# Raw weights staged a block earlier, v copied out before the last transpositions, score rows sent one transfer at a time

## The chip, the cores and the metric

The kernel runs on one core of a Trainium2 chip. The metric is the device time of one execution in microseconds (us); three timed runs of the kernel before gave 2346.47, 2347.64 and 2350.71 us, median 2347.64. A difference of about 0.2% (4.7 us) is what such a measurement can tell from no change.

The engines of the core are named as the profile names them: PE (matrix products; PEld its weight loads), DVE (vector), ACT (activations and copies), POOL, and SP, which here only issues transfers. ACT can issue transfers too, and an engine works through its own instructions in order, an issue among them.

## The reference

A gated sum of an attention block and a two-layer MLP on the same 2048 tokens of width 576, all in float32:

```python
x = A_x                                              # [1, 2048, 576]
g = sigmoid((x * gate_w).sum(-1, keepdims=True))
# attention, 32 heads of 18
q, k, v = split(x @ wqkv)
a = concat_heads(softmax(q @ k.T * 18 ** -0.5) @ v) @ wo
# MLP, hidden width 4608
y = layernorm(x)
b = gelu(y @ w1 + b1) @ w2 + b2
out = g * a + (1 - g) * b
```

## The kernel before

Matrix products run on float32 numbers split into a rounded high part and a rest (hi, lo), three products for one. The program has two parts.

**Opening, about 0 to 240 us.** Four token blocks of 512 tokens (`tb` 0 to 3) pass through a list `work` of 17 groups (13 in the last block): nine groups `qk_group` make q and k rows and store them to DRAM (`qk_scr`), eight groups `v_group` make v, copy it from PSUM into one of two tiles `VT` and store it (`v_scr`). Between the groups other work of the same block is placed by its number g in the list: `norm` at g = 2 to 5 (in block 0 from 5), `x_chunk` transposes the next block of x (g = 2 to 6), `y_chunk` transposes the normalised x of this block and stores it (from g = 11 in block 0, from 8 in blocks 1 and 2), and `load_x` fetches the block after next at the end. Rounds of first scores (`next_round`, line L201 on PE, L203 on DVE) begin in block 1. In the last block the last four v groups are computed side by side as `v_chunk` stages 0 to 3: each stage has matrix products into the four PSUM tiles `quad` (L907), then transpositions of normalised x (L911) whose results ACT and DVE split (L912, L913); after stage 3, `v_out` copies the four tiles out (L888 on ACT, L890 on DVE) and ACT itself issues the two stores (L891).

PSUM is shared: `transposed`, `v_chunk` and the rounds take turns in three buffers `ps_s1`, and the four banks of `ps_a` that the groups and `quad` use become `ps_s2` and `ps_w` afterwards, so the first MLP products (L474) write where `quad` was.

The MLP is a generator, `mlp()`, that is advanced by `next(stream[0])`. Its first four advances lie in block 3, at g = 2, 6, 9 and ahead of 13. The first loads raw weights into a tile `raws` of the x pool (L343, L345, L351), the second loads two more sets into the two tiles of the pool `pp` (`STAGED`), and the third splits them (ACT rounds at L374, POOL subtracts at L158). The tiles of `pp` are also the scratch (`junk`) that `norm` writes at g = 4 and 5 (L839).

**Loop, about 270 us to the end.** 32 units (pair of heads, half of the queries) of 16 steps. In each step PE makes scores (L244) into the single PSUM tile of `ps_s2`, ACT takes the exponential (L246), PE multiplies with v (L261); beside that run the rounds of the next unit, and MLP products (L474, L597) fill PE. The scheduler counts slots: `run_due` is called about four to five times a step, and `defer(n, fn)` runs fn n slots later. When the rounds of a unit are done, `s1_finish` makes four short rows of the maxima; `rows` turns them on PE (L218), ACT copies them (L220), and four transfers write them into `qa` (L113). They are issued by SP, except while SP is busy with the loads of the next block's y (`slot[0] < ybusy[0]`): then ACT issues all four, one behind the other.

Transfers take turns in eight completion counters, whichever engine issues them; an issue waits until the transfer that used its counter before has landed.

Of the kernel before, what the change touches and what calls it, by code (L numbers as in the profile page):

```python
# [16 lines left out]
P = 128  # L17
# [41 lines left out]
def gated_mix_kernel(ctx: ExitStack, tc: tile.TileContext, x, wqkv, wo, w1, b1, w2, b2, gate_w, out):  # L59
# [42 lines left out]
    def big_tile():  # L102
        return yp.tile([P, 9, TB], F32R, name="big")

    def x_tile():
        return xp.tile([P, 4 * 640], F32, name="x")
# [4 lines left out]
    def dma_r(queue, dst, src):  # L111

        queue.dma_start(dst.bitcast(F32), src)  # L113
# [91 lines left out]
    def s1_finish(u):  # L205

        m4 = M4.pop(u)
        nm = asm.tile([P, 2, 8], F32, name="nm")
        nm2 = asm.tile([P, 2, 2, 8], F32, name="nm2")
        nmh = asm.tile([P, 2, 8], F32R, name="nmh")  # L210
        nc.vector.tensor_reduce(nm, m4, axis=AX.X, op=ALU.max, negate=True)
        nc.vector.tensor_copy(nmh, nm)
        nc.vector.tensor_copy(nm2[:, :, 0, :], nmh.bitcast(F32))
        nc.vector.tensor_tensor(nm2[:, :, 1, :], nm, nmh.bitcast(F32), op=ALU.subtract)

        def rows():
            ps = psum(ps_s1)
            nc.tensor.transpose(ps[:32, :P], nm2.rearrange("p a b c -> p (a b c)"), ident)  # L218
            mr = asm.tile([32, P], F32R, name="mr", bufs=1)
            nc.scalar.activation(mr, ps[:32, :P], AF.Copy)  # L220
            qa = QA[u % 3]
            for h in range(2):
                for b in range(2):
                    r = 64 * h + 54 + b
                    k = (h * 2 + b) * 8
                    dma_r(nc.scalar if slot[0] < ybusy[0] else nc.sync,
                          qa[r:r + 1, :].rearrange("o (t n) -> o t n", n=P), mr[k:k + 8, :].bitcast(F32))
        if looped[0]:
            ROWS.append(rows)
        else:  # L230
            defer(9, rows)
# [76 lines left out]
    def mlp():  # L308
# [10 lines left out]
            return i, m, seq[i][1] * G + 2 * m  # L319


        raws = x_tile()
        R1 = raws[:, :9 * P].rearrange("p (c n) -> p c n", c=9)
        R2 = [raws[:, 9 * P + k * D:9 * P + (k + 1) * D] for k in range(2)]
        LOADED = {}
        STAGED = {}
        NQ0 = npair // NB

        def raw1(q):
            return STAGED.get((1, q), R1)  # L330

        def raw2(c):
            return STAGED[2, c] if (2, c) in STAGED else R2[c % 4]
# [13 lines left out]
        def load_w2(c):  # L347
            if (2, c) in LOADED or c >= NFC or c % 4 >= len(R2) and (2, c) not in STAGED:
                return
            LOADED[2, c] = slot[0] + (LAND - 4 if looped[0] else 4)  # L350
            nc.sync.dma_start(raw2(c), w2[c * P:(c + 1) * P, :])  # L351
# [277 lines left out]
                HT.pop((i, j))  # L629
                W2.pop((i * (G // 2) + j // 2, j % 2))  # L630

        load_w1(0)
        for c in range(2):
            load_w2(c)
        Y[0] = big_tile()
        yield 1
        for k in range(2):
            t = pp.tile([P, 2, 2, TB], F32, name="p").rearrange("p a b c -> p (a b c)")
            STAGED[1, 1 + k] = t[:, :9 * P].rearrange("p (c n) -> p c n", c=9)
            STAGED[2, 2 + k] = t[:, 9 * P:9 * P + D]  # L640
            load_w1(1 + k)
            load_w2(2 + k)
        yield 1
        prep(0)
        prep_w2(0)
# [81 lines left out]
    with ExitStack() as a:  # L727
# [85 lines left out]
        def norm(tb, stage):  # L813

            xv = x_view(tb)
            ts_ = slice(4 * tb, 4 * tb + 4)
            if stage < 2:
                for t in (2 * stage, 2 * stage + 1):
                    st6 = sm.tile([P, 2, nc.vector.BN_STATS_DIM], F32, name="st6")
                    for n in range(2):  # L820
                        nc.vector.bn_stats(st6[:, n, :], xv[:, t, n * ND:(n + 1) * ND])
                    nc.vector.bn_aggr(stats[:, tb * 4 + t, :], st6)
            if stage == 1:
                rstd = rstds[tb] = sm.tile([P, 4], F32, name="rstd")
                sd = sm.tile([P, 4], F32, name="sd")
                var = sm.tile([P, 4], F32, name="var")
                nc.vector.tensor_scalar(var, stats[:, ts_, 1], LN_EPS, None, op0=ALU.add)
                nc.scalar.activation(sd, var, AF.Sqrt)

                nc.vector.reciprocal(rstd, sd)  # L830
                nc.vector.tensor_mul(rstd, rstd, var)
                nc.vector.tensor_add(sd, sd, rstd)
                nc.vector.tensor_scalar(sd, sd, 0.5, None, op0=ALU.mult)
                nc.vector.reciprocal(rstd, sd)
            if stage >= 2:
                junk = pp.tile([P, 2, 2, TB], F32, name="p").rearrange("p a b c -> p (a b c)")
                for t in (2 * stage - 4, 2 * stage - 3):
                    tt = 4 * tb + t
                    nc.vector.scalar_tensor_tensor(junk[:, :D], xv[:, t, 0:D], 1.0, gwb, op0=ALU.mult, op1=ALU.mult,  # L839
                                                   accum_out=glog[:, tt:tt + 1])  # L840
                    if tb == NB - 1:
                        nc.vector.tensor_scalar(xv[:, t, D:], xv[:, t, 0:64], stats[:, tt, 0:1], rstds[tb][:, t:t + 1],
                                                op0=ALU.subtract, op1=ALU.mult)
                    xs = xv[:, t, 0:D]
                    nc.vector.tensor_scalar(xs, xs, stats[:, tt, 0:1], rstds[tb][:, t:t + 1],
                                            op0=ALU.subtract, op1=ALU.mult)
# [48 lines left out]
        def v_chunk(tb, stage):  # L895

            big = xT[tb]
            wh, wl = W_V
            if stage == 0:
                quad.extend(psum(ps_a) for _ in range(4))  # L900
            for c in ((0,), (1,), (2,), (3, 4))[stage]:
                for i, ps in enumerate(quad):
                    tok = slice((2 + i // 2) * P, (3 + i // 2) * P)
                    cs = slice(i % 2 * ND, (i % 2 + 1) * ND)
                    prods = ((c, wh), (c, wl), (4 + c, wh)) if c < 4 else ((8, wh), (8, wl))
                    for k, (s_, w_) in enumerate(prods):
                        nc.tensor.matmul(ps[:, :ND], big[:, s_, tok], w_[:, c, cs], start=(c == 0 and k == 0), stop=(c == 4 and k == 1))  # L907
                for cy in (c, 4 + c) if c < 4 else (8,):
                    ps = psum(ps_s1)
                    for t in range(4):  # L910
                        nc.tensor.transpose(ps[:, t * P:(t + 1) * P], x_view(tb)[:, t, 64 * cy:64 * cy + P], ident)  # L911
                    nc.scalar.activation(made[0][:, cy, :], ps, AF.Copy)  # L912
                    nc.vector.tensor_tensor(made[1][:, cy, :], ps, made[0][:, cy, :].bitcast(F32), op=ALU.subtract)  # L913
            if stage == 3:
                for i, ps in enumerate(quad):
                    v_out(tb, 2 + i // 2, i % 2, ps)

        load_w(0)
        load_x(0)
# [18 lines left out]
        for tb in range(NB):  # L938
# [3 lines left out]
            for g, (fn, args) in enumerate(work):  # L942
# [12 lines left out]
                ng = g - (N_AT if tb == 0 else 2)  # L955
                if 0 <= ng < 4:
                    norm(tb, ng)
                if tb + 1 < NB and 2 <= g < 7:
                    x_chunk(tb + 1, g - 2)
                yg = g - (11 if tb == 0 else 8)  # L960
                if 0 <= yg < 5 and tb < NB - 1:
                    y_chunk(tb, yg)
                if g == (16 if tb == 0 else 13) and tb + 2 < NB:
# [1 line left out]
                if tb == NB - 1:  # L965
                    if g == 1:
                        load_k(0, 3 * TB, S)
                    if g == 2:
                        load_q(1)
                        next(stream[0])  # L970
                    if g == 6:
                        next(stream[0])
                    if g == 9:
                        qkstack.close()
                        wp1 = mstack.enter_context(tc.tile_pool(name="m_w1", bufs=3))
                        wp2 = mstack.enter_context(tc.tile_pool(name="m_w2", bufs=4))
                        next(stream[0])

                        nc.scalar.activation(gate, glog, AF.Exp, scale=-1.0)
                    if g == 14:  # L980
                        nc.vector.tensor_scalar(gate, gate, 1.0, None, op0=ALU.add)
                        nc.vector.reciprocal(gate, gate)
                        nc.vector.tensor_scalar(gate1, gate, -1.0, 1.0, op0=ALU.mult, op1=ALU.add)
# [4 lines left out]
                    load_k(0, TB, 2 * TB)  # L988
                if tb == 2 and g == 3:
                    load_k(0, 2 * TB, 3 * TB)  # L990
                if tb == 2 and g == 13:
                    ps = psum(ps_s1)
                    nc.tensor.transpose(ps[:, :NFC], b1r, ident[:NFC, :NFC])
                    nc.vector.tensor_copy(b1t, ps[:, :NFC])
# [287 lines left out]
```

## Time and profile before

| what | value |
|---|---|
| timed runs, median (lowest to highest) | 2347.64 us (2346.47 to 2350.71) |
| the profiled execution, its own time | 2348.81 us |
| its span in the profile | 2347.0 us |
| mean granted PE clock | 0.996 |
| busy share PE / DVE / ACT / POOL | 98% / 71% / 59% / 40% |
| PE on the chain that ended last | 90% |
| DMA | 324.11 MB, mean 138 GB/s |

The span is what the profile covers; 1.8 us of the execution lie around it. PE is busy for nearly the whole span, but a busy PE may run at half clock, so the granted clock (PEclk) is read beside it. In the profile a row of the timeline gives start, duration, engine, line, operation and tiles, and in brackets the idle time ahead of it and what ended that.

### The profile page before, as it was taken

What the parts mean: (1) busy time and instruction counts of PE and PEld (TensorE: products, weight loads), DVE (VectorE), ACT (ScalarE), POOL (GpSimd) and SP (SyncE); (2) the same over time, 40 slices, a digit from 0 to 9 for tenths busy, and PEclk for the clock granted to TensorE, in tenths of its full rate; (3) what the DMA queues carried; (4) which work ended last, traced back from release to release, by engine and by line L of the source; (5) the groups of instructions that cost most, each with busy time, mean ns of one, the idle gap of its engine ahead of it and who ended that gap; (6) DMA issues with size and microseconds to landing.
All of it is one profiled execution on the core that took longest, in us unless ns stands there. A gap on an engine that the chain in (4) does not pass through costs nothing.

```text
span 2347.0 us, 50658 instructions
## 1 busy us (share of the span) xinstructions
PE 2299.5 (98%) x20601; PEld 1620.3 (69%) x20601; DVE 1661.0 (71%) x2920; ACT 1378.7 (59%) x1626; POOL 947.7 (40%) x936
## 2 busy tenths in 40 slices
PE   8999899999999999999999999999999999999999
PEld 6878666666676666666666666666666666666668
DVE  5674677777777777777767777777777777777645
ACT  4223576666665666666665666666666666666662
POOL 4002466555554433334352434443344444343320
PEclk9999999999999999999999999999999999999999
DMA  7746555545373524223364424242464333332346
GB/s 224 249 168 195 180 164 172 153 135 158 125 207 103 157 88 144 95 76 129 102 147 142 135 92 136 95 120 92 120 158 149 116 96 118 106 99 105 112 136 222
DMA packets 162078, 324.11 MB, mean 138 GB/s; under 512 B 58126, under 2 KB 85042, under 8 KB 151010
## 3 DMA queue, kind: packets, MB, share of 16 engines
q1 hardware_dynamic: 158006, 313.68, 42.6%
q10 hardware_dynamic: 3840, 7.19, 0.8%
q8 instruction: 162, 2.65, 0.5%
q14 instruction: 70, 0.57, 0.1%
HBM read 229.59 MB, written 95.16 MB: 138 GB/s over the span
## 4 chain that ended last, share of the span: by engine, by line
PE 90%; DVE 3%; DMA 2%; ACT 2%; issue 2%; POOL 1%; SPq 0%; ACTq 0%; DVEq 0%; POOLq 0%
PE ps L597 20%; PE ps L261 19%; PE ps L474 18%; PE pss L244 13%; PE ps L201 11%; PE ps L859 3%; PE ps L1160 3%; PE ps L877 1%; DVE m L203 1%; DMA x<-in_A_x_dram 1%; PE ps L777 1%; ACT p L246 0%; ACT w L374 0%; DVE p L839 0%; POOL w L158 0%
## 5 line engine op out<-in xcount | busy, mean ns | idle before, releaser
L203 DVE TENSOR_REDUCE m<-ps 128x1 f32<-128x512 f32 x2048 | 1296.6, 683 | 441.3 <-PE ps L201 440.7
L246 ACT ACTIVATE p<-pss 128x1024 f32<-128x1024 f32 x684 | 701.7, 1026 | 462.5 <-PE pss L244 448.6
L474 PE MATMUL ps<-big,w 64*128 64x512 f32 x3834 | 515.6, 393 | 2.6 <-ACT vt L888 2.6
L597 PE MATMUL ps<-w,hh 64*128 64x288 f32 x4352 | 499.4, 300 | 12.7 <-ACT z L497 0.8
L158 POOL TENSOR_SCALAR zz<-zz 128x512 f32<-128x512 f32 x272 | 169.2, 622 | 845.3 <-ACT zz L558 776.0
L244 PE MATMUL pss<-qa,ka 56*128 56x512 f32 x2048 | 482.6, 437 | 10.4 <-ACT p L246 6.3
L246 ACT ACTIVATE ring<-pss 128x1024 f32<-128x1024 f32 x340 | 348.9, 1026 | 232.7 <-PE pss L244 223.3
L201 PE MATMUL ps<-ka,qa 54*128 54x512 f32 x2048 | 456.1, 409 | 2.7 <-DVE m L203 1.6
L597 PEld LDWEIGHTS ps<-w,hh 64*128 64x128 f32 x4352 | 400.8, 186 | 68.5 <-issue 42.5
L474 PEld LDWEIGHTS ps<-big,w 64*128 64x128 f32 x3834 | 391.7, 185 | 60.8 <-ACT vt L888 2.9
L244 PEld LDWEIGHTS pss<-qa,ka 56*128 56x128 f32 x2048 | 196.8, 184 | 265.6 <-ACT p L246 132.1
L158 POOL TENSOR_TENSOR zz<-zz,z 128x512 f32<-128x512 f32 x280 | 361.3, 1291 | 38.9 <-ACT zz L560 13.9
L597 PE MATMUL ps<-w,hl 64*128 64x288 f32 x2176 | 350.3, 293 | 0.0
L261 PE MATMUL ps<-p,vt 128*32 128x512 f32 x2736 | 344.5, 598 | 0.0
L201 PEld LDWEIGHTS ps<-ka,qa 54*128 54x128 f32 x2048 | 242.3, 185 | 28.6 <-DVE m L203 9.1
L597 PEld LDWEIGHTS ps<-w,hl 64*128 64x128 f32 x2176 | 235.1, 186 | 0.4
L158 POOL TENSOR_TENSOR w<-x,w 128x576 fp32r<-128x576 f32 (+1 forms) x34 | 67.9, 2010 | 302.5 <-DMA p<-in_B_w_dram 168.7
L158 POOL TENSOR_TENSOR hl<-zz,hh 128x512 fp32r<-128x512 f32 x134 | 174.2, 1300 | 16.7 <-ACT hh L523 5.8
L261 PE MATMUL ps<-ring,vt 128*32 128x512 f32 x1360 | 179.1, 598 | 0.0
L261 PEld LDWEIGHTS ps<-p,vt 128*32 128x32 f32 x2736 | 71.4, 109 | 147.5 <-issue 147.5
L576 DVE SCALAR_TENSOR_TENSOR x<-ps,x 128x288 f32<-128x288 f32 x270 | 110.7, 452 | 30.9 <-PE ps L597 17.7
L859 PE MATMUL ps<-big,wqk 128*128 128x512 f32 x504 | 123.8, 400 | 1.5 <-DVE wqk L771 1.2
(121 smaller groups left out, 1402.4 us busy)
## 6 DMA issues: line engine op xcount, KB each, us to landing
w<-w_scr SPq DMA_DIRECT2D x54, 1152.0 KB
w<-w_scr SPq DMA_DIRECT2D x108, 576.0 KB
w_scr<-w SPq DMA_DIRECT2D x18, 1152.0 KB
w_scr<-w SPq DMA_DIRECT2D x36, 576.0 KB
qa<-qk_scr SPq DMA_DIRECT2D x192, 72.0 KB
ka<-qk_scr SPq DMA_DIRECT2D x90, 144.0 KB
x<-in_B_w_dram SPq DMA_DIRECT2D x34, 288.0 KB
qk_scr<-hh SPq DMA_DIRECT2D x36, 256.0 KB
```

Source lines behind the costliest of these rows:

```text
L158: fn(*args, **kw)
L201: nc.tensor.matmul(ps, qa[r0:r0 + 54, t * P:(t + 1) * P], ka[r0:r0 + 54, kb * TB:(kb + 1) * TB], start=True, stop=True)
L203: nc.vector.tensor_reduce(M4[u][:, h, t, kb:kb + 1], ps, axis=AX.X, op=ALU.max)
L244: nc.tensor.matmul(ps[:, h, :], ka[r0:r0 + 56, kc * P:(kc + 1) * P], qa[r0:r0 + 56, qb * TB:(qb + 1) * TB], start=True, stop=True)
L246: nc.scalar.activation(RING[n % 3][:, qb], ps, AF.Exp, scale=SCALE)
L261: nc.tensor.matmul(OB[u][r:r + 32, :], v[:, k, 19 * h:19 * h + 32], RING[c % 3][:, qb, h, :], start=(k == 0), stop=(k == NT - 1))
L474: nc.tensor.matmul(ps[h], wt[w_][r, c, :], Y[s_][r, c, :], start=(k == 0), stop=(k == 26))
L576: nc.vector.scalar_tensor_tensor(dst, ps[nn][:, :ND], 0.5, b2b[:, cs[nn]] if base else dst, op0=ALU.mult, op1=ALU.add)
L597: nc.tensor.matmul(ps[nn][:, :ND], h_[r, tok], w_[p_][r, cs[nn]], start=(k == 0 or bare and k == 3 * G), stop=(k == 6 * G - 1 or bare and ...
L777: nc.tensor.transpose(ps[:, t * P:(t + 1) * P], x_view(tb)[:, t, c * P:(c + 1) * P], ident)
L859: nc.tensor.matmul(ps, w_[:, c, ms], big[:, s_, :], start=(k == 0), stop=(k == len(prods) - 1))
L1160: nc.tensor.matmul(ps[t, n][:, :ND], OT[b][3][:, s_, tok], w_part(w_, c)[:, cs], start=(c == 0 and k == 0), stop=(c == 4 and k == 1))
```

## The change

Six edits go together.

1. The two sets of raw weights for `pp` are loaded by the first advance of `mlp()`, which moves to block 2, g = 6; the loads into `raws` come with the second advance, at block 3, g = 2, where they were. The advance at block 3, g = 6 is gone.
2. `norm` gets a scratch tile of its own (`junk`, in the pool `sm`), since the tiles of `pp` are now held from block 2 on.
3. In `v_chunk` stage 3, all products come first, then the four copies of `v_out`, then the last three transpositions.
4. The four row transfers that ACT issues are deferred to 1, 3, 5 and 7 slots later, one each. Those that SP issues stay together.
5. In block 1, `x_chunk` runs at g = 4 to 8 instead of 2 to 6.
6. In block 0, `y_chunk` runs from g = 12 instead of 11, so its last piece falls to the last group.

```diff
@@ s1_finish / rows
-            for h in range(2):
-                for b in range(2):
-                    r = 64 * h + 54 + b
-                    k = (h * 2 + b) * 8
-                    dma_r(nc.scalar if slot[0] < ybusy[0] else nc.sync,
-                          qa[r:r + 1, :].rearrange("o (t n) -> o t n", n=P), mr[k:k + 8, :].bitcast(F32))
+            aside = slot[0] < ybusy[0]
+
+            def store(h, b):
+                r = 64 * h + 54 + b
+                k = (h * 2 + b) * 8
+                dma_r(nc.scalar if aside else nc.sync,
+                      qa[r:r + 1, :].rearrange("o (t n) -> o t n", n=P), mr[k:k + 8, :].bitcast(F32))
+            for k in range(4):
+                if aside:
+                    defer(1 + 2 * k, lambda k=k: store(*divmod(k, 2)))
+                else:
+                    store(*divmod(k, 2))
@@ mlp
-        raws = x_tile()
-        R1 = raws[:, :9 * P].rearrange("p (c n) -> p c n", c=9)
-        R2 = [raws[:, 9 * P + k * D:9 * P + (k + 1) * D] for k in range(2)]
+        R1, R2 = {}, []
+
+        def open_raws():
+            raws = x_tile()
+            R1[0] = raws[:, :9 * P].rearrange("p (c n) -> p c n", c=9)
+            R2.extend(raws[:, 9 * P + k * D:9 * P + (k + 1) * D] for k in range(2))
...
-        load_w1(0)
-        for c in range(2):
-            load_w2(c)
-        Y[0] = big_tile()
-        yield 1
         for k in range(2):
             t = pp.tile([P, 2, 2, TB], F32, name="p").rearrange("p a b c -> p (a b c)")
             STAGED[1, 1 + k] = t[:, :9 * P].rearrange("p (c n) -> p c n", c=9)
             STAGED[2, 2 + k] = t[:, 9 * P:9 * P + D]
             load_w1(1 + k)
             load_w2(2 + k)
+        yield 1
+        open_raws()
+        load_w1(0)
+        for c in range(2):
+            load_w2(c)
+        Y[0] = big_tile()
         yield 1
@@ norm
-                junk = pp.tile([P, 2, 2, TB], F32, name="p").rearrange("p a b c -> p (a b c)")
+                junk = sm.tile([P, D], F32, name="junk", bufs=1)
@@ v_chunk
-            for c in ((0,), (1,), (2,), (3, 4))[stage]:
+            cs_ = ((0,), (1,), (2,), (3, 4))[stage]
+            for c in cs_:
                 for i, ps in enumerate(quad):
...
+            if stage == 3:
+                for i, ps in enumerate(quad):
+                    v_out(tb, 2 + i // 2, i % 2, ps)
+            for c in cs_:
                 for cy in (c, 4 + c) if c < 4 else (8,):
...
-            if stage == 3:
-                for i, ps in enumerate(quad):
-                    v_out(tb, 2 + i // 2, i % 2, ps)
@@ the loop over token blocks
-                if tb + 1 < NB and 2 <= g < 7:
-                    x_chunk(tb + 1, g - 2)
-                yg = g - (11 if tb == 0 else 8)
+                xg = g - (4 if tb == 1 else 2)
+                if tb + 1 < NB and 0 <= xg < 5:
+                    x_chunk(tb + 1, xg)
+                yg = g - (12 if tb == 0 else 8)
...
-                        next(stream[0])
-                    if g == 6:
                         next(stream[0])
...
+                if tb == 2 and g == 6:
+                    next(stream[0])
```

**ACT at the end of block 3.** These are the rows of ACT before, from the last rounding of a staged weight (`w<-p`) to the first MLP row (`z<-ps,b1t`):

```order
94 L374 ACTIVATE w_2201<-p 128x1152
95 L912 ACTIVATE big<-ps 128x512 x3
96 L888 ACTIVATE vt_109<-ps 128x8x2x18
97 L891 DMA v_scr<-vt_109 128x832
98 L888 ACTIVATE vt_110<-ps 128x8x2x18
99 L891 DMA v_scr<-vt_110 128x832
100 L497 ACTIVATE z<-ps,b1t 128x512
```

And the same place in the changed program, whose line numbers are some ten higher:

```order
94 L383 ACTIVATE w_2201<-p 128x1152
95 L898 ACTIVATE vt_109<-ps 128x8x2x18
96 L901 DMA v_scr<-vt_109 128x832
97 L898 ACTIVATE vt_110<-ps 128x8x2x18
98 L901 DMA v_scr<-vt_110 128x832
99 L927 ACTIVATE big<-ps 128x512 x3
100 L506 ACTIVATE z<-ps,b1t 128x512
```

The two copies of v and their stores stand ahead of the three copies of transposed x instead of behind them; the rounding of the staged weights has not moved.

**ACT in the loop, where it issues the rows.** Before, at the first of the two places where this happens (`mr` holds the rows, `pss` the scores):

```order
382 L220 ACTIVATE mr<-ps 32x128
383 L113 DMA qa_104<-mr 1x8x128 x4
384 L246 ACTIVATE p<-pss 128x1024 x3
385 L246 ACTIVATE ring_2263<-pss 128x1024 x2
386 L374 ACTIVATE w_8752<-x 128x576
```

And after the change:

```order
382 L220 ACTIVATE mr<-ps 32x128
383 L113 DMA qa_104<-mr 1x8x128
384 L252 ACTIVATE p<-pss 128x1024
385 L113 DMA qa_104<-mr 1x8x128
386 L252 ACTIVATE p<-pss 128x1024
387 L113 DMA qa_104<-mr 1x8x128
388 L252 ACTIVATE p<-pss 128x1024
389 L113 DMA qa_104<-mr 1x8x128
390 L252 ACTIVATE ring_2263<-pss 128x1024 x2
```

One transfer now stands ahead of each of four exponentials. Of the eight exponentials of these four steps seven follow `mr` before the unit that needs the rows begins, so the last transfer is issued four exponentials, two steps, ahead of that.

More of the change, by code (lines that the diff above doesn't have):

```diff
@@ L329, in raw1 @@
         def raw1(q):
-            return STAGED.get((1, q), R1)
+            return STAGED[1, q] if (1, q) in STAGED else R1[0]
         def raw2(c):
@@ L835, in norm @@
             if stage >= 2:
-                junk = pp.tile([P, 2, 2, TB], F32, name="p").rearrange("p a b c -> p (a b c)")
+                junk = sm.tile([P, D], F32, name="junk", bufs=1)
                 for t in (2 * stage - 4, 2 * stage - 3):
                     tt = 4 * tb + t
-                    nc.vector.scalar_tensor_tensor(junk[:, :D], xv[:, t, 0:D], 1.0, gwb, op0=ALU.mult, op1=ALU.mult,
+                    nc.vector.scalar_tensor_tensor(junk, xv[:, t, 0:D], 1.0, gwb, op0=ALU.mult, op1=ALU.mult,
                                                    accum_out=glog[:, tt:tt + 1])
```

## The prediction

> **What bounds the kernel now.** I read the page's totals first, then who PE waited for, then the timeline around each long wait, then the granted clock in short windows behind them.
>
> ```profile
> span 2347.0 us, 50658 instructions
> PE 2299.5 (98%) x20601; PEld 1620.3 (69%) x20601; DVE 1661.0 (71%) x2920; ACT 1378.7 (59%) x1626; POOL 947.7 (40%) x936
> ...
> PE ps L777 <- DMA x<-in_A_x_dram: 8.7, 3, 6.0
> PE pss L244 <- ACT p L246: 6.3, 7, 2.2
> PE ps L911 <- DVE big L913: 3.2, 1, 3.2
> PE ps L474 <- ACT vt L888: 2.6, 1, 2.6
> ```
>
> PE is busy for 2299.5 of 2347.0 us, and the work on it does not change: the same products and transpositions in a slightly different order. So the change can win only from PE's 47.5 idle us and from time in which PE runs slowly. The waits (us in total, times, longest) name only a handful of stalls over 2 us; apart from the first 6.0 us, ahead of all work, the diff bears on each of the long ones. The sum is therefore one over stalls, each with the slow clock behind it. The columns of these windows are the window, its length, busy us of PE, PEld, DVE, ACT and POOL, then the granted PE clock, the DMA share and GB/s:
>
> ```profile
> 227.00:232.00 5.00, 4.93 (x27) 4.92 (x28) 3.49 (x8) 2.60 (x5) 2.94 (x2) 0.66 1.03 287
> 238.00:242.00 4.00, 3.62 (x18) 2.92 (x20) 0.23 (x1) 0.33 (x1) 0.00 (x0) 0.57 0.54 213
> 272.00:280.00 8.00, 7.82 (x55) 6.21 (x57) 4.38 (x8) 5.58 (x9) 3.81 (x3) 0.57 0.55 80
> 712.00:717.00 5.00, 4.91 (x41) 3.91 (x42) 2.07 (x5) 1.98 (x3) 0.00 (x0) 0.66 0.00 0
> 1219.00:1224.00 5.00, 4.91 (x56) 3.37 (x58) 2.96 (x6) 4.11 (x5) 2.85 (x4) 1.00 0.62 152
> ```
>
> Length times (1 - clock) is the time lost: 5 x 0.34 = 1.70, 4 x 0.43 = 1.72, 8 x 0.43 = 3.44, 1.70 and 0 us. The first two windows follow the stalls at 224 and 236 us, the fourth the one at 709; behind that at 1217 nothing was lost.
>
> **Part 1: raw weights loaded in block 2 (with the scratch tile).** The stall at 224 us:
>
> ```profile
> SPq L343 <- DMA v_scr<-vt: 7.3, 1, 7.3
> ...
> 211.35 8.54 SPq L343 DMA_DIRECT2D p<-in_B_w_dram  x2
> 220.81 1.03 PE L911 MATMUL ps<-ident,x 128*128 128x128 f32 x8
> ...
> 225.12 0.68 ACT L374 ACTIVATE w<-p 128x576 fp32r<-128x576 f32 x1 [6.25 <-DMA p<-in_B_w_dram]
> 225.71 1.07 ACT L912 ACTIVATE big<-ps 128x512 fp32r<-128x512 f32 x2
> 226.32 1.29 DVE L913 TENSOR_TENSOR big<-ps,big 128x512 fp32r<-128x512 f32 x2 [6.47 <-ACT big L912]
> 227.07 0.66 PE L911 MATMUL ps<-ident,x 128*128 128x128 f32 x4 [3.19 <-DVE big L913]
> ```
>
> SP hung 8.54 us in the second staged set behind a v store; the set came late; ACT stood 6.25 us in the rounding L374, with the copies L912 queued behind; DVE and, for a free `ps_s1` buffer, PE waited for those. With the loads some 60 us earlier ACT waits for nothing here. What is late next: the buffer PE wants needs L912 and L913 of the first transpositions, 1.07 + 1.29 us behind the transpositions that start at 220.81, so about 223.5, and PE comes at 223.88 (227.07 - 3.19). So the whole 3.19 us go, and the 1.70 us of clock behind: **4.9 us** (from 0 if another wait takes the place, to 4.9).
>
> In their new place the eight loads stand on SP between the q and k stores of block 2:
>
> ```profile
> 136.00:160.00 24.00, 23.03 (x96) 15.89 (x95) 21.20 (x47) 5.72 (x11) 0.00 (x0) 1.00 0.30 109
> ...
> 210.00 0.62 SPq L345 DMA_DIRECT2D p<-in_B_w_dram  x1
> ...
> p<-in_B_w_dram SPq DMA_DIRECT2D x4, 288.0 KB
> p<-in_B_w_dram SPq DMA_DIRECT2D x2, 256.0 KB
> ...
> 121.66 3.46 PE ps L859 x14
> 182.54 9.80 PE ps L859 x42
> ```
>
> DMA is busy for 0.30 there. Both sets are about 1.7 MB (4 x 288 + 2 x 256 KB and two small ones); at the 287 GB/s of the window 227 to 232 that is 6 us of transfers. Eight issues at about 0.6 us are 5 us on SP. Behind them wait the stores of the next groups, whose source tiles rotate in six. Block 2 lasts from 121.66 to 182.54 (first products of blocks 2 and 3 on the chain) and takes 14 such tiles, one in 4.3 us, so a store may be some 26 us late before ACT, then PE, feels it. Cost 0, up to 5 if SP's issues were exposed. The scratch tile is written by the same DVE rows: 0.
>
> **Part 2: v copied out before the last transpositions.**
>
> ```profile
> 233.21 1.03 PE L911 MATMUL ps<-ident,x 128*128 128x128 f32 x8
> ...
> 235.14 0.60 PE L911 MATMUL ps<-ident,x 128*128 128x128 f32 x4
> ...
> 236.27 0.41 ACT L888 ACTIVATE vt<-ps 128x288 f32<-128x288 f32 x1
> ...
> 237.91 0.42 ACT L888 ACTIVATE vt<-ps 128x288 f32<-128x288 f32 x1 [1.23 <-issue]
> 238.38 2.93 PE L474 MATMUL ps<-big,w 64*128 64x512 f32 x12 [2.64 <-ACT vt L888]
> ```
>
> PE is done at 235.74 and waits until ACT's second copy ends at 238.33, because L474 writes the bank that this copy reads. ACT had to do the last three L912 first, then a copy, an issue that waits for DVE's copy, and the second copy: 2.06 us from 236.27. After the change that same 2.06 us chain starts when the first `quad` tile is complete, six products before PE ends them, and PE still has twelve transpositions to make, 1.03 + 0.60 = 1.6 us. Six products at the transpositions' pace (1.03 / 8 = 0.13 us) are 0.8 us, so the second copy lands some 1.3 us after PE's last product, inside the 1.6. L912 now comes behind, but L474 takes the transposed pieces in order and needs the late ones only after twelve of its products (2.93 x 0.57 = 1.7 us at full clock). So 2.64 + 1.72 = **4.4 us** (0 to 4.4).
>
> **Part 3: rows one at a time.**
>
> ```profile
> L113 ACTq DMA_DIRECT2D qa<-mr x8: 627/630/1225, 706.7 to 1217.0; - x8
> ...
> 706.72 3.27 ACTq L113 DMA_DIRECT2D qa<-mr  x4
> 710.03 1.02 ACT L246 ACTIVATE p<-pss 128x1024 f32<-128x1024 f32 x1 [3.34 <-DMA qa<-mr]
> 711.11 0.50 PE L244 MATMUL pss<-qa,ka 56*128 56x512 f32 x2 [2.23 <-ACT p L246]
> ...
> 1217.64 1.02 ACT L246 ACTIVATE ring<-pss 128x1024 f32<-128x1024 f32 x1 [2.74 <-DMA qa<-mr]
> 1218.72 0.51 PE L244 MATMUL pss<-qa,ka 56*128 56x512 f32 x2 [2.20 <-ACT ring L246]
> ```
>
> ACT issues rows at only these two places, eight transfers in all, at 0.63 us each but for the first. Four in a row hold an exponential 3.34 and 2.74 us, and PE, with one score tile, 2.23 and 2.20 us. One issue ahead of each exponential holds it 0.63 us at most. PE's slack there is 3.34 - 2.23 = 1.1 us at the first place, so nothing is left; at the second it is 2.74 - 2.20 = 0.54, so 0.1 remains for the first issue, and 0.2 or so for each of the other three, which also share ACT with the tanh rows: 0.6. Gain 2.23 + 1.70 and 2.20 - 0.6: **5.5 us** (bounds 0 and 6.1). The 512 steps fill the span from about 270 us on, 4.0 us each, with two exponentials: the last row leaves three exponentials or 6 us later than now, and the unit that reads it begins four exponentials or 8 us after that, which a transfer of a few KB should not need. A transfer that ACT issues must also find its completion counter free; for seven of the eight the one before is long landed, and the last follows a y load issued some 10 us before.
>
> **Part 4: the two shifts in blocks 0 and 1.**
>
> ```profile
> 52.70 0.33 PE L777 MATMUL ps<-ident,x 128*128 128x128 f32 x1 [0.35 <-DVE x L845]
> 53.99 0.33 PE L777 MATMUL ps<-ident,x 128*128 128x128 f32 x1 [0.96 <-DVE x L845]
> ...
> 76.57 0.66 PE L777 MATMUL ps<-ident,x 128*128 128x128 f32 x4 [1.44 <-DMA x<-in_A_x_dram]
> ...
> 91.45 0.60 PE L777 MATMUL ps<-ident,x 128*128 128x128 f32 x4
> ...
> 93.99 0.69 DVE L795 TENSOR_TENSOR big<-ps,hh 64x512 fp32r<-64x512 f32 x1
> ```
>
> One v group more ahead of the transpositions (fourteen products at 0.13 us, 1.8 us) covers the 0.35 + 0.96 us but for 0.1: gain 1.2. Two groups later (2 x 3.46 us by the row of block 2 above) x has landed: gain 1.44. The load of x for block 2 now waits for one more transposition, and goes out about 1 us later; 7 us cover that. But the last `x_chunk` of block 1 now shares g = 8 with the first `y_chunk` and a round: four tiles in three buffers. The fourth waits for L795, 93.99 + 0.69 - 91.45 = 3.2 us after its transposition in this row, where DVE was still on `norm`; I take 2.3 without that (the 1.07 + 1.29 us of two such copies and a subtraction), against 1.3 us of PE work between (two transposition rows and a product). That is 1.05 (0 to 1.9). Sum of part 4: **+1.6 us** (0.7 to 2.6).
>
> **The sum.** 4.9 + 4.4 + 5.5 + 1.6 = 16.4 us. From the profiled execution's 2348.81 us that leaves 2332.4. The median of the timed runs is 1.2 us below that execution, about what one more or less slow stretch costs, so I forecast **2332 us** for the median.
>
> [...]
>
> **The rivals.**
> - *The clock does not come back.* The slow stretches may hang on where a stall falls; the one at 272 us stands behind no wait of over 2 us, and all stages there move by some 11 us. Then the 1.70 + 1.72 + 1.70 = 5.1 us stay, here or elsewhere: 2348.8 - 11.3 = 2337.5. The three that follow stalls speak against it. The same doubt works downward: without the 272 us stretch it is 2332.4 - 3.4 = 2329.
> - *A new wait takes the place at 224 us.* ACT could stand in the rounding of the sets that still load in block 3, or POOL's subtractions be late for L474. For it: those loads stay on a busy SP. Against: ACT did not wait for them before. Loses part 1: 2337.3.
> - *The rows do nothing*, as each single issue still hits an exponential without slack: 4 x 0.63 us lost at each place again. Loses part 3: 2337.9.
> - *Slower: SP jams in block 2.* If the eight loads held SP so long that the six rotating tiles run out, ACT, then PE, would stall there. It decides from 26 us of hold on, and to end above 2352.3 it must add some 20 us beyond: 46 us. SP's longest hold of this kind was 8.54 us with DMA at 1.0; here DMA is at 0.30.
>
> **How the numbers follow.** The forecast, all parts within their bounds (2328.5 to 2335.5): 0.50. Clock stays: 0.20. New wait: 0.12. Rows: 0.06. Several of these together, leaving less than 4.7 us (0.2%, about what a measurement can tell from no change): 0.07. Slower: 0.05. Faster is 0.50 + 0.20 + 0.12 + 0.06 = 0.88. The range 2328 to 2340 takes in the first four cases, with a little lost at each edge.
>
> **What would show it.** Right: no PE wait of L911 on L913, none of L474 on L888, none over 0.5 us of L244 near 707 and 1215 less the shift; no L374 behind a transfer; x landed ahead of L777; clock 1.0 around the v chunks. Wrong: an L374 row that still names a transfer, an L201 in block 1 waiting far over 1 us, SP rows of many us at 150, or new stretches of clock 0.5.

## The result, and the profile after

Six timed runs of the changed kernel gave a median of 2333.31 us (2332.89 to 2333.87), six of the kernel before beside them 2347.65 us (2346.47 to 2350.71): ratio 0.9934, 95% interval 0.9924 to 0.9943, so 14.3 us or 0.6% faster. The profiled execution took 2333.75 us (span 2332.0), 15.06 us less than that of before. The runs also scatter less: 1.0 us from lowest to highest instead of 4.2.

The page's totals of the changed kernel, then who PE waited for (us in total, times, longest):

```profile
span 2332.0 us, 50662 instructions
...
PE 2295.1 (98%) x20601; PEld 1613.1 (69%) x20601; DVE 1661.4 (71%) x2920; ACT 1378.4 (59%) x1626; POOL 947.8 (41%) x936
```

```profile
PE ps L787 <- DMA x<-in_A_x_dram: 7.3, 2, 6.2
PE pss L250 <- ACT p L252: 4.3, 7, 1.1
PE ps L201 <- DVE m L203: 1.6, 1, 1.6
...
PE ps L201 <- DVE big L805: 1.1, 1, 1.1
...
PE ps L1173 <- DVE big L1113: 0.6, 1, 0.6
```

No wait of over 2 us is left but the first load, and the transpositions' wait for DVE and that of the MLP's first product for `vt` are gone. One wait of 1.1 us is new (L201 on L805, block 1). Where the time came from, by the starts of the same instructions in the two profiled executions:

| place | before | after | gained so far |
|---|---|---|---|
| first product of block 1 | 65.18 | 63.44 | 1.74 |
| first product of block 2 | 121.59 | 119.90 | 1.69 |
| first MLP product (L474, now L483) | 238.38 | 229.14 | 9.24 |
| maxima turned (L218), first place of the rows | 706.10 | 695.96 | 10.14 |
| the same, second place | 1214.28 | 1200.53 | 13.75 |
| end of the span | 2347.0 | 2332.0 | 15.0 |

The end of the attention opening, in the timeline of the changed kernel:

```profile
217.08 0.67 ACT L383 ACTIVATE w<-p 128x576 fp32r<-128x576 f32 x1
...
224.86 2.90 PE L918 MATMUL ps<-wv,big 128*128 128x288 f32 x20
...
227.00 0.42 ACT L898 ACTIVATE vt<-ps 128x288 f32<-128x288 f32 x1 [0.15 <-PE ps L918]
227.60 1.47 PE L926 MATMUL ps<-ident,x 128*128 128x128 f32 x12
228.67 0.42 ACT L898 ACTIVATE vt<-ps 128x288 f32<-128x288 f32 x1 [1.25 <-PE ps L926]
229.14 1.66 PE L483 MATMUL ps<-big,w 64*128 64x512 f32 x12
...
230.87 1.09 PE L201 MATMUL ps<-ka,qa 54*128 54x512 f32 x2
```

The rounding of the staged weights (L383) waits for nothing. The second copy of v ends at 229.09, 1.33 us behind the last product (224.86 + 2.90 = 227.76), and PE transposes until 229.07: L483 starts at 229.14, with no margin to spare. One pair of score products at 230.87 then takes 1.09 us, where such a pair takes 0.40 elsewhere.

The staged loads in their new place, on SP in block 2:

```profile
153.01 2.57 SPq L352 DMA_DIRECT2D p<-in_B_w_dram  x2
...
156.98 1.29 SPq L352 DMA_DIRECT2D p<-in_B_w_dram  x2
...
158.99 0.58 SPq L360 DMA_DIRECT2D p<-in_B_w_dram  x1
```

They hold SP from 153.01 to 159.57, 6.6 us in all and 2.57 at most, far from the 26 us of cover; PE waits for nothing new there. The rows in the loop, ACT first, then PE at the two places:

```profile
696.58 1.23 ACTq L113 DMA_DIRECT2D qa<-mr  x1
697.86 1.03 ACT L252 ACTIVATE p<-pss 128x1024 f32<-128x1024 f32 x1 [1.31 <-PE ps L201]
697.89 0.67 ACTq L113 DMA_DIRECT2D qa<-mr  x1
699.48 1.02 ACT L252 ACTIVATE p<-pss 128x1024 f32<-128x1024 f32 x1 [0.59 <-PE pss L250]
699.49 0.63 ACTq L113 DMA_DIRECT2D qa<-mr  x1
...
698.94 0.50 PE L250 MATMUL pss<-qa,ka 56*128 56x512 f32 x2 [0.19 <-ACT p L252]
...
1202.97 0.50 PE L250 MATMUL pss<-qa,ka 56*128 56x512 f32 x2 [0.20 <-ACT ring L252]
```

PE's 2.23 and 2.20 us have become 0.19 and 0.20. Behind the second place 15.8 us were gained (a score row at 1204.94 for 1220.71); the end gives 0.8 back, and the new wait of L1173 is 0.6 us.

The granted clock (last columns: clock, DMA share, GB/s) behind the old stalls, and where it is still low:

```profile
227.00:232.00 5.00, 4.77 (x35) 3.54 (x35) 3.41 (x8) 2.42 (x5) 2.57 (x1) 1.00 0.43 170
...
261.00:269.00 8.00, 7.03 (x43) 5.56 (x43) 4.21 (x9) 5.88 (x9) 3.81 (x3) 0.57 0.70 106
701.00:706.00 5.00, 5.00 (x52) 3.04 (x50) 3.77 (x7) 2.74 (x3) 0.00 (x0) 1.00 0.00 1
```

Three of the four slow stretches are gone; the fourth (8 x 0.43 = 3.4 us) only moved, from 272 to 261 us. It stands in every profile of this study.

### The profile page after: what moved, and what is told of

Its sections match the earlier page's. It is cut to its first block, busy times and chain, and to the rows that moved or that the text cites. A ratio compares the mean times of both kernels' runs of the same rounds, so it can differ in the third digit from the quotient of the medians.

```text
span 2332.0 us, 50662 instructions
## 1 busy us (share of the span) xinstructions
PE 2295.1 (98%) x20601; PEld 1613.1 (69%) x20601; DVE 1661.4 (71%) x2920; ACT 1378.4 (59%) x1626; POOL 947.8 (41%) x936
## 4 chain that ended last, share of the span: by engine, by line
PE 92%; DVE 2%; issue 2%; ACT 2%; DMA 1%; POOL 1%; ACTq 0%; SPq 0%; DVEq 0%; POOLq 0%
PE ps L606 20%; PE ps L267 20%; PE ps L483 18%; PE pss L250 13%; PE ps L201 11%; PE ps L869 4%; PE ps L1173 2%; PE ps L887 2%; DVE m L203 1%; PE ps L787 0%; ACT p L252 0%; ACT w L383 0%; DMA x<-in_A_x_dram 0%; PE ps L918 0%; POOL w L158 0%
## 5 line engine op out<-in xcount | busy, mean ns | idle before, releaser
L483 PE MATMUL ps<-big,w 64*128 64x512 f32 x3834 | 514.5, 392 | 0.1
L201 PE MATMUL ps<-ka,qa 54*128 54x512 f32 x2048 | 457.8, 409 | 4.0 <-DVE m L203 1.6
L483 PEld LDWEIGHTS ps<-big,w 64*128 64x128 f32 x3834 | 388.7, 185 | 59.9 <-ACT vt L898 0.3
L201 PEld LDWEIGHTS ps<-ka,qa 54*128 54x128 f32 x2048 | 243.2, 185 | 31.3 <-DVE m L203 8.9
L585 DVE SCALAR_TENSOR_TENSOR x<-ps,x 128x288 f32<-128x288 f32 x270 | 110.7, 451 | 29.6 <-PE ps L606 16.4
```

The costliest lines, as they stand in the source:

```text
L201: nc.tensor.matmul(ps, qa[r0:r0 + 54, t * P:(t + 1) * P], ka[r0:r0 + 54, kb * TB:(kb + 1) * TB], start=True, stop=True)
L483: nc.tensor.matmul(ps[h], wt[w_][r, c, :], Y[s_][r, c, :], start=(k == 0), stop=(k == 26))
L585: nc.vector.scalar_tensor_tensor(dst, ps[nn][:, :ND], 0.5, b2b[:, cs[nn]] if base else dst, op0=ALU.mult, op1=ALU.add)
```

## The experiments

Medians in us, the number of runs, and the kernel before on the same chip beside them. That figure names three groups of measurements (2346.77, 2347.37 and 2348.77 us); it differs by 2 us between them, so across groups the ratios are compared:

| run | kernel | median (runs) | before (runs) | ratio, 95% |
|---|---|---|---|---|
| e1_rows | before + rows one at a time | 2341.66 (11) | 2346.77 (33) | 0.9975 [0.9966, 0.9984] |
| e2_stage | before + staging in block 2 | 2344.17 (11) | 2346.77 (33) | 0.9990 [0.9981, 0.9999] |
| e3_vout | before + v copied out earlier | 2345.52 (11) | 2346.77 (33) | 0.9993 [0.9985, 1.0002] |
| e4_shift | before + the two shifts | 2347.33 (11) | 2346.77 (33) | 1.0000 [0.9991, 1.0008] |
| e8_both | before + staging + v | 2341.31 (10) | 2347.37 (15) | 0.9972 [0.9963, 0.9982] |
| e5_rows_back | changed - rows | 2340.02 (6) | 2347.37 (15) | 0.9969 [0.9957, 0.9980] |
| e10_v_back | changed - v | 2335.88 (5) | 2347.37 (15) | 0.9953 [0.9941, 0.9966] |
| e11_stage_back | changed - staging | 2337.00 (5) | 2347.37 (15) | 0.9957 [0.9943, 0.9970] |
| e12_shift_back | changed - shifts | 2334.82 (5) | 2348.77 (9) | 0.9939 [0.9926, 0.9953] |
| e6_x3 | changed, x one group earlier | 2331.46 (5) | 2348.77 (9) | 0.9927 [0.9915, 0.9939] |
| e9_stalls | changed + 28 stalls | 2474.41 (1) | | |

### One part alone, on the kernel before

Each takes one part of the diff shown above as it stands. e1_rows, the rows:

```diff
...
+            for k in range(4):
+                if aside:
+                    defer(1 + 2 * k, lambda k=k: store(*divmod(k, 2)))
...
```

> The kernel before with only the rows aside going one transfer at a time. My theory (a stall of 2.2 us of PE at each of two places, one of them with 1.7 us of slow clock behind it): 5.5 us faster, about 2342 us, no score product waiting over 0.5 us near 707 and 1215 us. Rival (each single issue holds its exponential as the four did): 0 us, about 2347.6. Middle (the waits go but the slow clock turns up elsewhere): 3.8 us faster.

5.1 us faster; no score product waits over 0.5 us at either place, and no slow clock stands there. As expected.

e2_stage, the staging and the scratch tile:

```diff
...
+                if tb == 2 and g == 6:
+                    next(stream[0])
...
+                junk = sm.tile([P, D], F32, name="junk", bufs=1)
```

> The kernel before with only the raw weights staged in block 2 and the scratch tile of its own. My theory: the 3.19 us stall at 224 us and the 1.70 us of clock behind it go, 4.9 us faster, about 2342.7 us; the stall at the v copies (2.6 us) stays. Rival 1 (another wait takes the place): 0. Rival 2 (the slow clock stays, since the stall at the v copies follows 12 us later and may catch it): 3.2 us faster.

2.6 us faster by the medians (interval 0.2 to 4.5), about half of what was expected. In its profile the stall at 224 us is gone and the one for `vt` stays (2.64 us) with a slow stretch behind it; the first MLP product comes at 232.88, 5.5 us earlier than before, of which 0.9 were already gained at the start of block 3, where x landed earlier in that execution.

e3_vout, v's copies:

```diff
...
+            if stage == 3:
+                for i, ps in enumerate(quad):
+                    v_out(tb, 2 + i // 2, i % 2, ps)
             for c in cs_:
...
```

> The kernel before with only v's last copies ahead of the last transpositions. My theory: 2.64 us of stall and 1.72 us of clock go, 4.4 us faster, about 2343.3 us; the stall of the transpositions at 224 us (3.2 us) stays. Rival (ACT, late from the late weights, is still behind, so the first product of attention waits for its copies or the transposed pieces all the same): 0 to 2 us.

1.25 us faster, which can't be told from none. The wait for `vt` is gone, that of the transpositions stays (2.5 us) with its slow stretch, and this profile has another stall near the end (1.85 us, L1162 on DVE) with 1.7 us of clock behind it. That wait has 0.6 us in the changed kernel's profile and 1.0 in e6_x3; no edit bears on it.

e4_shift, the shifts:

```diff
+                xg = g - (4 if tb == 1 else 2)
+                if tb + 1 < NB and 0 <= xg < 5:
+                    x_chunk(tb + 1, xg)
+                yg = g - (12 if tb == 0 else 8)
```

> The kernel before with only the two shifts in blocks 0 and 1. My theory: 1.2 us in block 0 and 1.44 in block 1, less a new wait of about 1.1 us for a fourth score tile: 1.6 to 1.9 us faster, about 2346 us. Rival (everything behind moves against the clock's window, and slow stretches come or go): anything from 2 us slower to 5 us faster, with the waits after 200 us as before.

0.6 us slower, with an interval of 2 us to either side: inconclusive. Its block 1 starts at 63.41 as in the changed kernel, and it has the new wait of 1.1 us.

The four add up to 5.1 + 2.6 + 1.25 - 0.6 = 8.4 us, not 14.3. Each bears an error of about 2 us, since the kernel before scatters by 6.6 us over its 33 runs. Whether the rest is error or the parts help each other was the next question.

### Two parts together, and the changed kernel without one part

e8_both joins the edits of e2_stage and e3_vout; the others take one part out of the changed kernel, where the base is steady.

```diff
...
+                if tb == 2 and g == 6:
+                    next(stream[0])
...
+            if stage == 3:
+                for i, ps in enumerate(quad):
+                    v_out(tb, 2 + i // 2, i % 2, ps)
```

> The kernel before with two parts together: the raw weights staged in block 2 (with the scratch tile), and v's last copies ahead of the last transpositions. Alone they gave 2.6 and 1.25 us by the medians. If the parts simply add up as measured alone: 3.9 us faster, about 2343. My theory (each alone leaves the other's stall, with 1.7 us of slow clock behind it for certain, and together there is no stall left between 200 and 240 us): 9.3 us by the prediction's terms, 8.2 by the places of the changed kernel's rows, about 2338.5.

6.1 us faster (interval 4.2 to 8.7). That lies between the 3.9 of the two alone and my 8.2; the interval takes in 8.2, and the 3.9 have an error of some 3 us, so the run does not decide between them. Its profile has no stall and no slow clock between 200 and 240 us.

e10_v_back undoes the edit of e3_vout:

```diff
...
-            if stage == 3:
-                for i, ps in enumerate(quad):
-                    v_out(tb, 2 + i // 2, i % 2, ps)
...
```

> The changed kernel with v's last copies behind the last transpositions again. Theory: 2.64 us of stall and 1.7 us of clock come back: 4.4 us slower than the changed kernel, about 2337.7. Rival (the parts only add what they add alone): 1.3 us slower, 2334.6.

2.6 us slower than the changed kernel by the medians, between the two expectations. The stall is back to the digit (its row of the timeline), but no slow clock follows it (windows of 3.41 us: length, busy PE, PEld, DVE, ACT and POOL, clock, DMA share, GB/s):

```profile
231.80 1.67 PE L483 MATMUL ps<-big,w 64*128 64x512 f32 x12 [2.64 <-ACT vt L898]
```

```profile
227.32:230.73 3.41, 1.83 (x16) 1.59 (x13) 2.51 (x5) 1.69 (x4) 1.99 (x1) 1.00 0.00 0
230.73:234.15 3.42, 2.35 (x20) 1.95 (x22) 0.93 (x3) 0.42 (x1) 0.00 (x0) 1.00 0.63 249
```

e11_stage_back undoes the edits of e2_stage:

```diff
...
-                if tb == 2 and g == 6:
-                    next(stream[0])
```

> The changed kernel with all raw weights loaded in block 3 again, and the scratch in the shared buffer. Theory: the stall of the transpositions on DVE's subtractions comes back with 2.5 to 4.1 us, as in the profiles of the kernel before and of three experiments, and 1.7 us of clock: 4.2 to 5.8 us slower than the changed kernel, about 2338.3. Rival (the parts only add what they add alone): 2.6 us slower, 2336.

3.7 us slower by the medians. Its profile, 2.3 us above its median, has a stall of 3.65 us (timeline) and half clock in two windows behind it:

```profile
225.63 1.11 PE L922 MATMUL ps<-ident,x 128*128 128x128 f32 x4 [3.65 <-DVE big L924]
```

```profile
221.19:224.60 3.41, 0.79 (x7) 0.55 (x5) 0.00 (x0) 0.92 (x2) 0.80 (x2) 1.00 0.86 300
224.60:228.01 3.41, 2.38 (x11) 2.39 (x12) 2.39 (x4) 2.77 (x5) 2.79 (x2) 0.50 0.86 233
228.01:231.43 3.42, 3.42 (x17) 3.40 (x17) 1.85 (x5) 0.66 (x2) 1.11 (x1) 0.50 0.66 246
```

SP stands 7.88 us in the second staged set there, as it stood 8.54 us before. The trace shows what held it (timeline, then SP's waits):

```profile
209.46 7.88 SPq L349 DMA_DIRECT2D p<-in_B_w_dram  x2
...
214.32 0.35 ACTq L897 DMA_DIRECT2D v_scr<-vt  x1
```

```profile
SPq L349 <- DMA v_scr<-vt: 6.7, 1, 6.7
```

The second transfer of that row waits for the completion counter that the v store of ACT uses. ACT issues this store only at 214.32; its last packet lands at 216.73, and SP goes on at 216.75. Before it is the same: issued at 216.22, landed at 219.28, SP at 219.30. So SP stood behind a counter that came free late, in a window with a DMA share of 0.74 before, not behind full queues.

e5_rows_back undoes the edit of e1_rows:

```diff
...
-                if aside:
-                    defer(1 + 2 * k, lambda k=k: store(*divmod(k, 2)))
...
```

> The changed kernel with the four rows issued in a row again. Theory (a stall of 2.2 us at each of two places, slow clock of 1.7 us behind the first only, as in all five profiles that have these stalls): 5.6 us slower than the changed kernel, about 2339, and the slow stretch stands behind the first place again, not the second. Rival (the slow clock hangs on where a stall falls against a free-running window): 4 to 7.6 us, and either place may have it.

6.7 us slower by the medians. Both stalls are back, and here the slow clock stands behind both places, which refutes my theory that it belongs to the first (timeline, then windows):

```profile
700.62 0.79 PE L244 MATMUL pss<-qa,ka 56*128 56x512 f32 x2 [2.24 <-ACT p L246]
...
1208.20 0.50 PE L244 MATMUL pss<-qa,ka 56*128 56x512 f32 x2 [2.21 <-ACT ring L246]
```

```profile
697.24:700.65 3.41, 1.17 (x17) 0.83 (x14) 1.99 (x4) 1.02 (x1) 2.66 (x3) 1.00 0.04 10
700.65:704.07 3.42, 3.33 (x22) 2.80 (x24) 0.00 (x0) 1.02 (x1) 0.00 (x0) 0.50 0.00 0
1205.82:1209.24 3.42, 1.21 (x14) 0.89 (x12) 1.41 (x3) 1.52 (x2) 1.88 (x2) 1.00 0.65 134
1209.24:1212.65 3.41, 3.33 (x26) 3.02 (x26) 1.29 (x2) 2.26 (x4) 2.11 (x3) 0.50 0.64 168
```

e12_shift_back undoes the edits of e4_shift:

```diff
-                xg = g - (4 if tb == 1 else 2)
-                if tb + 1 < NB and 0 <= xg < 5:
-                    x_chunk(tb + 1, xg)
+                if tb + 1 < NB and 2 <= g < 7:
+                    x_chunk(tb + 1, g - 2)
-                yg = g - (12 if tb == 0 else 8)
+                yg = g - (11 if tb == 0 else 8)
```

> The changed kernel without the two shifts in blocks 0 and 1. By the places of the rows: block 1 starts 1.7 us later again, the transpositions of block 1 wait 0 to 1.5 us for x (0, 0.5, 0.7, 1.4 and 1.5 us in the five profiles that have this order), and the 1.1 us wait of the score product goes: 0.6 to 2.1 us slower than the changed kernel, about 2334.6. Rival (the shifts bring nothing, as their run alone had it): 0.

1.5 us slower by the medians, as expected, though the intervals of the two ratios overlap. Taken out one at a time the parts are worth 3.7 + 2.6 + 6.7 + 1.5 = 14.5 us by the medians, against 14.3 for the whole. These medians come from different groups; by the ratios, each against the kernel before beside it, they are 5.4 + 4.5 + 8.2 + 1.2 = 19.3 us against 15.5, each with an error of some 3 us. So taken out one at a time the parts add up within their errors. Put in alone they give 9.9 us by the ratios, 5.6 less than the whole, which is about the combined error of these five figures (some 5 us). Whether the parts help each other by a few us thus stays open.

### How long a stall slows the clock

e9_stalls repeats exponentials at 28 steps; `full` and `half` come from a list of seven sizes.

```diff
         nc.scalar.activation(RING[n % 3][:, qb], ps, AF.Exp, scale=SCALE)
+        full, half = STALLS.get((n, qb), (0, 0))
+        for _ in range(full):
+            nc.scalar.activation(RING[n % 3][:, qb], ps, AF.Exp, scale=SCALE)
+        if half:
+            nc.scalar.activation(RING[n % 3][:, qb, 0], ps[:, 0], AF.Exp, scale=SCALE)
```

> The changed kernel with exponentials computed a second to sixth time at 28 places among the 512 steps, so that the score product behind them waits; nothing else changes, and the values stay the same. An extra exponential takes ACT about 1.0 us, half of one 0.6, and PE has about 1.1 us of slack, so seven sizes of stall of about 1.0, 1.5, 2.0, 2.6, 3.0, 3.6 and 4.0 us come four times each. Theory A (a stall of over about 2 us can be followed by 1.7 us of half clock, by where it falls against a free-running window; the longer, the likelier): none behind 1.0 and 1.5 us, some behind 2.0 to 3.0, all or nearly all behind 3.6 and 4.0. [...] Theory C (it hangs on the place in the program, not on length): no order by length. Time: the stalls add some 70 us and the clock 1.7 us for each slow stretch.

The stalls came out longer than planned, 0.73 to 4.99 us and 93 us in all; the time was 2474.41 us in a single execution, 141 us more than the changed kernel's profiled execution. What stood behind each:

| stall, us | number | no slow clock | one slow window | two slow windows |
|---|---|---|---|---|
| 0.73 to 1.90 | 4 | 4 | | |
| 2.21 to 2.95 | 8 | 2 | 5 | 1 |
| 3.33 to 3.42 | 4 | | 4 | |
| 3.76 to 4.00 | 4 | | 1 | 3 |
| 4.32 to 4.99 | 8 | | | 8 |

That is theory A in its order, and more exact: in this run the granted 0.50 comes in whole windows of 3.41 us. By that, as an estimate, a window that is busy throughout loses 1.71 us, and what is idle in it loses nothing. PE was busy for 97.0 of the 116.1 us of the slow windows, so the clock cost 48.5 us and not 58. With it the time closes: PE's idle time rose by 92.3 us and its busy time by 48.3, together the 141. A second slow window followed where the stall reached at least 0.60 us into the first (all 12 cases), and none where it reached at most 0.32 us into it (the other 10). All 22 slow stretches begin on one grid with a period of 3.413 us, over 1090 us of execution, within 0.05 us. Cut along that grid, three stalls of 2.51, 2.36 and 3.89 us read:

```profile
1238.94:1242.35 3.41, 1.84 (x16) 1.39 (x14) 2.73 (x5) 2.82 (x3) 0.00 (x0) 1.00 0.51 107
1242.35:1245.77 3.42, 2.48 (x20) 1.64 (x24) 0.56 (x1) 2.17 (x4) 0.00 (x0) 1.00 1.00 367
1522.25:1525.66 3.41, 1.57 (x20) 1.22 (x16) 2.82 (x5) 3.20 (x4) 3.16 (x5) 1.00 0.22 50
1525.66:1529.08 3.42, 2.82 (x18) 2.38 (x20) 0.00 (x0) 1.49 (x2) 0.62 (x1) 0.50 0.44 129
...
1689.50:1692.91 3.41, 0.00 (x0) 0.00 (x0) 0.84 (x2) 3.31 (x4) 0.00 (x0) 1.00 0.00 0
1692.91:1696.33 3.42, 3.34 (x16) 2.68 (x18) 0.00 (x0) 1.05 (x2) 0.00 (x0) 0.50 0.00 0
```

The first window is idle for 3.41 - 1.84 = 1.57 us, and the next runs at full clock; the third is idle for 1.84 us, and the next runs at half. Among all full-speed windows of this stretch none idle up to 1.57 us was followed by half clock, and all from 1.84 us on were. (In the other profiles windows with up to 1.65 were not and those with 1.74 in e2_stage and 1.75 in e8_both were; against this order one with 1.57 in e4_shift was, so the records leave the limit open by some 0.1 us. The stretch near 261 us is left aside here.) So a stall cost clock here where about 1.7 us of it, half a window, fell into one window of the grid. From that limit I estimate that a stall of d us between 1.7 and 3.4 costs clock at a share d / 3.41 of its positions on the grid, which is 0.75 at 2.55 us: six of the eight from 2.21 to 2.95 had it.

The two places of the kernel before, on that execution's own grid:

```profile
709.29:712.70 3.41, 1.50 (x16) 1.23 (x18) 0.71 (x2) 2.05 (x2) 1.26 (x1) 1.00 0.02 3
712.70:716.12 3.42, 3.42 (x30) 3.25 (x28) 1.29 (x2) 1.02 (x1) 0.00 (x0) 0.50 0.00 0
1214.46:1217.87 3.41, 2.05 (x21) 1.61 (x20) 2.48 (x4) 0.67 (x3) 3.16 (x4) 1.00 1.06 229
1217.87:1221.28 3.41, 2.48 (x28) 2.12 (x30) 0.36 (x1) 2.46 (x4) 0.89 (x2) 1.00 0.26 56
```

At the first the stall puts 1.91 idle us into one window, at the second only 1.36, as it is cut in two. e10_v_back's two windows above, with 1.58 and 1.07 idle us, are the same case.

### Block 1's transpositions of x one group earlier

The new wait of 1.1 us in block 1 comes from four score tiles in one group with three buffers. One group earlier for `x_chunk` avoids it:

```diff
-                xg = g - (4 if tb == 1 else 2)
+                xg = g - (3 if tb == 1 else 2)
```

> The changed kernel with block 1's transpositions of x one group earlier (groups 3 to 7, not 4 to 8), so that no group has four score tiles to share three buffers. Theory: the wait of 1.1 us of a score product on a subtraction goes, and x has landed in time all the same: 1.1 us faster than the changed kernel, about 2332.2. Rivals: x comes late again (up to 0.5 us lost of it), or the wait moves to another group: 0.

2331.46 us (2331.15 to 2332.42), 1.85 us below the changed kernel's median with no overlap of their runs, though these come from different groups and the intervals of their ratios overlap. Within its own group it is 3.4 us below e12_shift_back, the same kernel without the shifts, with no overlap. Its waits have no L201 on L805, x landed in time, and block 2 starts at 118.20 instead of 119.90. So the places show the 1.1 us as gained; the times alone do not prove it against the changed kernel. The place in the changed kernel, then in this one:

```profile
96.26 0.50 PE L201 MATMUL ps<-ka,qa 54*128 54x512 f32 x1
97.88 0.50 PE L201 MATMUL ps<-ka,qa 54*128 54x512 f32 x1 [1.12 <-DVE big L805]
```

```profile
95.66 0.60 PE L787 MATMUL ps<-ident,x 128*128 128x128 f32 x4
96.19 0.49 PE L201 MATMUL ps<-ka,qa 54*128 54x512 f32 x2
```

## Why the prediction held, point by point

- **The whole.** From the profiled execution 16.4 us were to go and 15.06 went; the median came out 1.3 us above the 2332 of the forecast, whose step from 2332.4 takes off only 0.4 of the 1.2 us that it names. A sum over a handful of stalls with their clock was the right account: busy PE fell by 4.4 us (2299.5 to 2295.1), idle PE by 10.6 (47.5 to 36.9). In the timed runs the mean granted clock rose from 0.9966 (33 runs) to 0.9983 (6 runs), some 4 us of 2347, against 5.1 in the sum.
- **Part 1, 4.9 us.** The stall and its slow clock went, nothing took the place, and SP had room. Taken back it costs 3.7 us. The prediction's reading of SP's hold was off: the DMA share over those 8.54 us is 0.74, not 1.0, and the hold was a wait for a completion counter. The term rested on one execution: the same stall measures 3.19 us there and 2.49, 2.51, 3.65 and 4.10 in four others.
- **Part 2, 4.4 us.** The chain ran as worked out: the second copy lands 1.33 us behind the last product (predicted 1.3), but PE's transpositions end 1.31 us behind it instead of 1.6, so the stall is gone with nothing in hand. Taken back it costs 2.6 us, about the stall alone: the 1.72 us of clock behind it were there in three of the five profiles that have this stall (2.64 us each time), not always. This is the term that was mis-sized.
- **Part 3, 5.5 us.** 3.6 and 2.0 us at the two places by the table of places, 5.1 us alone, 6.7 when taken back. The clock behind the first place was counted as certain and behind the second as nothing; it is a matter of the grid at both. With it in six of six profiles at the first and one of six at the second, the sum came out right by luck, for a reason that I did not have. The 0.6 us kept for exposed issues was too much: PE waits 0.20.
- **Part 4, 1.6 us.** 1.5 when taken back, but by other pieces: block 0 gave 1.74 instead of 1.2 us (the 1.8 us of products there were enough for the whole 1.31, with no 0.1 to take off); the 1.44 us wait for x in block 1 was one of six outcomes from 0 to 1.53 (mean 0.8); the new wait cost 1.12 (1.05 predicted). The shift in block 1 as written thus gains nothing; one group earlier it does.
- **The rivals.** The clock came back to full at each of the three places, so the first falls, in its form that slow stretches move elsewhere; its doubt, that they hang on where a stall falls, was right. No new wait came at 224 us, the rows did bring their gain, and SP did not jam. The shortcoming is the clock's price: 1.7 us or nothing by chance, not 1.7 for sure.

## What to carry to other kernels

Where one engine is busy for 98% of the span, list its few stalls of over 2 us and find for each what stands ahead of the awaited operation on its engine; that is what to move. Price a stall in full, and the slow clock behind it by the chance that enough of it falls into one window of the clock's grid (here, by e9_stalls, an estimated d / 3.41 for a stall of d us between 1.7 and 3.4; the stretch near 261 us aside, no full-speed window of any profile with under 1.57 idle us had half clock behind it). Where runs scatter, judge small parts by taking them out of the steadier kernel, and measure what is compared side by side.

## What was not expected of the hardware

- The clock's grid: in e9_stalls all 22 slow stretches begin on one grid of 3.413 us over 1090 us of the execution. Its full-speed windows with up to 1.57 idle us were followed by full clock, those with 1.84 us and more by a granted 0.50, for one or two whole windows. The remaining slow stretch near 261 us does not fit: it follows windows with only 0.3 to 1.3 idle us by the records of the profiles. A row ahead of it in the changed kernel shows six score products as 3.30 us, where three pairs take 1.2 elsewhere, so part of the busy time may be waiting. That stays open.
- In the changed kernel ACT's issues run beside its own exponentials: the issue at 697.89 starts 0.03 us behind the exponential at 697.86, which takes 1.03 us. Issues that alternate with exponentials left PE waits of 0.19 and 0.20 us here; four in a row held an exponential for 3.34 us in the kernel before.
- The runs of the changed kernel spread over 1.0 us, those of the kernel before over 4.2 (6 runs) to 6.6 us (33). Stalls that put about 1.57 to 1.84 idle us into one window of the grid are one likely cause, but not shown to be the cause: e5_rows_back has two stalls of 2.2 us and spreads over 1.4 us, e10_v_back and e11_stage_back have one each and spread over 3.1 and 3.2.
